# Input transfers of 88 and 40 rows padded to 96 and 48, in a one-core mLSTM and MoE kernel with a planned instruction order

## The chip, the core and the metric

The kernel runs on one core of a Trainium2 chip. It is one launch; the metric is the device time of that launch in microseconds (us). A profiled execution gives, beside its time, the span from its first to its last instruction.

## What is computed

The reference is a chain of an mLSTM layer (32 heads of 40 dimensions, 768 steps, 4 batches) and two feed-forward blocks on the 3,072 tokens that it yields.

```
for t in range(S):
    m_new = max(f_gate[t] + m, i_gate[t]); f_stab = exp(f_gate[t] + m - m_new); i_stab = exp(i_gate[t] - m_new)
    C = f_stab * C + i_stab * outer(v_t, k_t);  n = f_stab * n + i_stab * k_t
    y[t] = sigmoid(o_gate[t]) * (C q_t) / max(|n . q_t|, 1)
x = y as (3072, 320)
x = ((x @ w1) * (x @ w2)) @ w3 @ w_out                      # 320 -> 1024 -> 1024 -> 320
out = max(x @ v1, x @ v2, x @ v3) @ v_out                   # 320 -> 768 -> 320
```

Everything is float32 to the caller.

## The kernel before

**Work.** The recurrence is cut into nine chunks of 88 steps (the last has 64) per batch, and each chunk into two units of four heads: 72 units, `u` from 0 to 71. A unit loads keys and values (`kv`, line 490), values shifted for the carried state (`vs`, line 493), queries and keys for the scores (line 528 for the first `NP` = 10 units, tile `raw`; line 531 for the others, tile `misc` in the trace), queries for the carried state (`qq`, line 535) and a row of decays spread over the partitions (`dd`, line 538). Every second unit also loads output gates (`og`: line 462 for the first five chunks, tile `sg`; line 504 afterwards). GpSimd (POOL) and ScalarE (ACT) make the decay matrix `dd` (lines 544 to 552); TensorE makes scores (line 568 in the first ten units straight from `raw`, line 589 in the others from rounded halves); VectorE multiplies them with `dd` into `pk` (line 599); POOL or VectorE scales `qq` into rows 64 to 127 of `pk` (line 595); TensorE multiplies `pk` with `kv` (line 609). Rows 88 to 127 of a `kv` tile carry the state; columns 0 to 39 of these rows hold an identity, put into each of the three `kv` buffers once by the transfers of line 455 from `eyes`. Rows 64 to 127 of each `qq` and `vs` buffer are set to zero once.

**Weights.** The weights come as 64-bit floats and are turned into 32-bit ones on the chip, a piece of 128 x 512 at a time (`granule`, transfers of line 831, ACT lines 836, 842 and 853, VectorE lines 845 and 859). `w3 @ w_out` is folded into one matrix (line 909). The feed-forward steps are long rows of matmuls (lines 681 to 685 and 748 to 767) over blocks of 384 tokens.

**Order.** Nothing is issued in the order of the program text. `Plan.op` records each operation with its engine, an estimate of its duration, what it reads and what it writes; `Plan.run` works through a model of the engines and fixes one order for all of them. An operation's rank is its latest start plus a bias for its engine and the first tile it writes (`BIAS`, "Dkv" is a DMA into `kv`). All transfers are issued by SyncE (SP), one queue in order; in the model each takes 450 ns of SP, then its estimate times a factor on a common bus, and no transfer is issued while the bus is more than `AHEAD` = 2,500 ns ahead of the clock. The order on each engine is then fixed; on the chip an engine works through it and waits at each instruction for what that needs. Semaphore waits are put in for every pair of accesses to the same rows of a tile.

**Lines the change touches.** Lines 450 to 453 copy, by ACT, an identity into columns 176 to 215 of each of the three `raw0` buffers. In line 533 `rs`, the number of score rows, is 88 for all units (`Q0` holds units 2 to 17, and units 0 and 1 have 88 rows anyway), so the four matmuls of line 568 read the 88 key columns of `raw` and not the identity behind them. The transfer of line 528 fills columns 0 to 175 of each head's 216, so that its pieces lie apart in the tile: 704 bytes each, four per partition.

Of the kernel before, what the change touches and what calls it, by code (L numbers as in the profile page):

```python
# [8 lines left out]
F32 = mybir.dt.float32  # L9
# [19 lines left out]
Q0 = tuple(range(2, 18))  # L29
# [20 lines left out]
BIAS = {"Add": -69250, "Aev": -20750, "Ag": -87500, "Akst": -433250, "Aph": -85750, "Aqs": -169250,  # L50
        "Araw0b": -112500, "Asa": 80250, "Asg": 77000, "Astg": 121500, "Asx": 172500, "Awa": 53750,
        "Awar": -227750, "Awb": -299750, "Awc": -44250, "Awcr": -22750, "Awd": -95750, "Axh": -106000,
        "Dcs": -153000, "Ddd": 56000, "Ddna": 41500, "Dev": 135250, "Dg": -568250, "Dkv": 58750,
        "Dkvb": -138750, "Dqq": -150000, "Draw": 61250, "Dsg": -172250, "Dstg": 56250, "Dsx": -253500,
        "Dvs": 54000, "Gdd": 165250, "Gg": 165750, "Gmp": -83500, "Gpk": -8500, "Gpl": 102000, "Gqqb": -89000,
        "Gqs": -328250, "Gvsb": -67000, "Gwa": 248750, "Gwar": 130750, "Gwc": 173750, "Gwcr": 276500,
        "Gwd": 10000, "Gy": -204000, "Pac0": 26000, "Pac1": -256750, "Pac2": -108750, "Po": -750, "Ppt": 32000,
        "Ps": -74250, "Pwk": 16250, "Pxt": -36000, "S-": -191250, "Sg": -328500, "Vam": -7250, "Vev": 440250,
        "Vg": -40750, "Vkst": 79750, "Vkv": -170750, "Vmp": -182500, "Vpk": -130500, "Vsa": -42250,
        "Vsg": -18250, "Vstg": 206750, "Vsx": 16750, "Vwb": -33250, "Vxl": 65500, "Vy": -8500, "Vzero": -40750}  # L60
# [21 lines left out]
class Plan:  # L82
# [48 lines left out]
    def run(self):  # L131
# [70 lines left out]
        while events:  # L202
# [22 lines left out]
            for e, h in heaps.items():  # L225
                while h and free[e] <= t:
                    j = h[0][1]
                    if done[j]:
                        heapq.heappop(h)
                        continue  # L230
                    if e == "D" and bus > t + AHEAD:
                        push(-1, bus - AHEAD)
                        break
                    heapq.heappop(h)
                    done[j] = True
                    a = ops[j][0].index(e)
                    ns = ops[j][1][a]
                    order.append((t, j, ops[j][2][a]))
                    if e == "D":
                        free[e] = t + 450  # L240
                        bus = max(bus, t + 1300) + ns * 1.4
                        end = bus + 1200
                    elif e == "P":
                        free[e] = end = clock(t, ns, self.cols[j])
                        past.append((t, end, self.cols[j]))
                    else:
                        end = t + ns
                        if e == "G" or e == "V" and self.port[j]:
                            at = t + GRAB[e]
                            x, y = held["V" if e == "G" else "G"]  # L250
                            if x <= at < y:
                                end = y + ns - GRAB[e]
                            held[e] = (at, end)
                        free[e] = end
                    for key, s in touch[j]:
                        if key not in part:
                            part[key] = 0
                            use[s][0] += 1
                        part[key] += 1
                        use[s][1] = max(use[s][1], end + 250)  # L260
# [15 lines left out]
def mlstm_moe_kernel(  # L276
# [45 lines left out]
    for pool_, tag, bufs, n in (  # L322
# [3 lines left out]
        (tmp, "sx", EX, 1024), (tmp, "w3", L_BUFS, 512), (tmp, "raw0", RAW0, 4 * (128 + L)),  # L326
# [123 lines left out]
    eye = cs[0:40, 0:40].unsqueeze(1).to_broadcast([40, 4, 40])  # L450
    for i, t in enumerate(slots["raw0"]):
        P.op("A", act(160), lambda t=t: A.copy(out=view(t, [40, 4, 128 + L], F32)[:, :, 2 * L:128 + L], in_=eye),
             r=[("cs", 0)], w=[("raw0b", i)])
# [7 lines left out]
    for c in range(SIGN):  # L461
        dma(313, lambda c=c: SP.dma_start(out=sg0[0:L, c], in_=og[0, c]), w=[("sg", (0, c))])
        sig.append(P.op("A", 360 + (1283 if c == 0 else 0), lambda c=c: A.activation(
            out=sg0[0:L, c], in_=sg0[0:L, c], func=AF.Sigmoid
        ), w=[("sg", (0, c))]))
# [19 lines left out]
    def load(u):  # L485
# [4 lines left out]
        dma(317, lambda: SP.dma_start(out=T("kv", u)[0:L], in_=kv[b, g, c]), w=[("kv", u, "k")])  # L490
        if c:
            new(("vs", u), [128, 4, 41], F32, "vs")
            dma(44, lambda: SP.dma_start(out=T("vs", u)[64:L].rearrange("p a b -> p (a b)"), in_=vs[b, g, c]),
                r=[("vsb", turn["vs"] % len(slots["vs"]))], w=[("vs", u)])

    def gates(b, c):
# [25 lines left out]
    def unit(u):  # L522
# [3 lines left out]
        if u < NP:  # L526
            new(("raw", u), [40, 4, L + 128], F32, "raw0")
            dma(313, lambda: SP.dma_start(out=T("raw", u)[:, :, 0:2 * L], in_=qk0[g, c]), w=[("raw", u)])
        else:
            new(("raw", u), [120, 2, 4, L], F32, "raw")  # L530
            dma(939, lambda: SP.dma_start(out=T("raw", u), in_=qk[b, g, c]), w=[("raw", u)])
        rs = L if u >= NP or u in Q0 else r
        if rs < r:
            new(("qq", u), [128, 4, L], F32, "qq")
            dma(157, lambda: SP.dma_start(out=T("qq", u)[L:128], in_=qk[b, g, c, 0:40, 0]),
                r=[("qqb", turn["qq"] % len(slots["qq"]))], w=[("qq", u)])
        new(("dd", u), [128, 4, n], F32, "dd")
        dma(501, lambda: SP.dma_start(
# [24 lines left out]
        if u < NP:  # L563

            def f():
                raw = T("raw", u)
                for h in range(4):
                    PE.matmul(T("s", u)[:rs, h], lhsT=raw[:, h, L:L + rs], rhs=raw[:, h, 0:n], start=True, stop=True)

            P.op("P", 870 if rs == 128 else 640, f, r=[("raw", u), ("raw0b", u % RAW0)], w=[("s", u)])  # L570
# [21 lines left out]
        if rs < r:  # L592
# [7 lines left out]
            out=T("pk", u)[:rs, :, 0:n], in0=T("s", u)[:rs], in1=T("dd", u)[:rs], op=ALU.mult  # L600
# [217 lines left out]
    def granule(src, dst=None):  # L818
# [12 lines left out]
        dma(n * 2.844, lambda: SP.dma_start(out=tl().rearrange("p a b -> p (a b)"), in_=src.bitcast(I32)),  # L831
# [218 lines left out]
def _lay(i):  # L1050
# [9 lines left out]
    qk0 = qk0.reshape(2, NCH, D, 4, 2 * L)  # L1060
    qk = np.concatenate([qk, qk[:, :, :, 0:24], qk, qk[:, :, :, 24:40]], 3)
    kvt = np.zeros((B, 2, NCH, L, 4, 81), f)
    kk = k.reshape(B, 2, 4, S, D).transpose(0, 1, 3, 2, 4)
    vv = v.reshape(B, 2, 4, S, D).transpose(0, 1, 3, 2, 4)
    kvt[:, :, :, :, :, 80] = 1.0
# [4 lines left out]
    og = np.zeros((B, NCH, L, DM), f)  # L1070
# [55 lines left out]
```

## Time and profile before

| | |
|---|---|
| median of 3 runs | 735.6 us (735.3 to 739.76) |
| the profiled execution | 736.07 us |
| its span | 733.5 us |
| TensorE (PE) busy | 693.9 us, 95% of the span |
| weight loads (PEld) / VectorE (DVE) / ACT / POOL busy | 667.0 / 493.4 / 361.3 / 359.8 us |
| moved by DMA | 80.43 MB |

The page gives busy time by engine and 40 slices of the span, then the DMA queues, the chain of work that ended last, and the costliest groups of instructions. Views of the trace ask the same of a stretch, a line or a tile. A wait is the idle time of an engine before an instruction, with the event that ended it. The granted clock is TensorE's: 1.00 stands for 2.4 GHz, 0.50 for 1.2 GHz, and a value between is a mean over a stretch that holds both.

### The profile page before, as it was taken

The numbers are of one execution on the slowest core, as the hardware profiler recorded it, in microseconds if no ns is written. First come the engines' busy times: TensorE is split into PE (matmuls) and PEld (weight loads), VectorE is DVE, ScalarE is ACT, GpSimd is POOL, SyncE is SP. The second block draws the span as 40 slices with busy tenths as digits, with TensorE's granted clock in tenths as the row PEclk, the third lists the DMA queues.
The fourth block names the chain that finished last, engine by engine and source line by source line (L and its number), as shares of the span: only waits on it lengthen the run. The fifth ranks groups of instructions, "written<-read, shape, count | busy, mean of one in ns | idle before, by whom it ended". The sixth has DMA issues, their size and how long they took to land.

```text
span 733.5 us, 12870 instructions
## 1 busy us (share of the span) xinstructions
PE 693.9 (95%) x4269; PEld 667.0 (91%) x4269; DVE 493.4 (67%) x1202; ACT 361.3 (49%) x722; POOL 359.8 (49%) x494
## 2 busy tenths in 40 slices
PE   0788799999999999999999999999999999999998
PEld 0576787889899999999999999999999999999997
DVE  6578798897887788677575687776476783233333
ACT  7769799978984334353242334453233232322221
POOL 2587587877746457765342467865144441000000
PEclk9968799999999999999999999999999999999999
DMA  6887678765542435432221354433032320000000
GB/s 193 253 236 223 204 192 234 225 202 149 170 144 79 111 89 156 109 100 81 61 59 46 107 127 133 121 103 85 11 84 82 89 69 1 1 0 1 1 28 27
DMA packets 50994, 80.43 MB, mean 110 GB/s; under 512 B 10881, under 2 KB 37153, under 8 KB 50929
## 3 DMA queue, kind: packets, MB, share of 16 engines
q1 hardware_dynamic: 50928, 79.62, 38.6%
q8 instruction: 33, 0.54, 0.3%
q14 instruction: 33, 0.26, 0.1%
HBM read 75.57 MB, written 4.03 MB: 109 GB/s over the span
## 4 chain that ended last, share of the span: by engine, by line
PE 79%; DVE 7%; ACT 7%; issue 2%; DMA 2%; POOL 1%; SPq 1%; DVEq 0%; ACTq 0%; POOLq 0%
PE wk L681 12%; PE wk L683 12%; PE wk L682 12%; PE ac L767 8%; PE aq L609 6%; PE wk L685 6%; PE wk L684 6%; PE ac L748 4%; PE ac L752 4%; PE wk L909 3%; PE ac L750 2%; PE aq L589 2%; ACT stg L853 2%; PE aq L649 1%; ACT stg L836 1%
## 5 line engine op out<-in xcount | busy, mean ns | idle before, releaser
L697 ACT CAST ph<-pr 128x384 fp32r<-128x384 f32 (+1 forms) x114 | 58.0, 510 | 115.2 <-PE ac L767 43.8
L701 POOL TENSOR_TENSOR pl<-pr,ph 128x384 fp32r<-128x384 f32 (+1 forms) x52 | 53.1, 1021 | 124.1 <-ACT ph L697 106.1
L732 DVE TENSOR_TENSOR pr<-pr,wk 128x384 f32<-128x384 f32 (+1 forms) x98 | 52.4, 537 | 70.1 <-PE wk L685 68.5
L681 PE MATMUL wk<-xh,wch 128*128 128x384 f32 x288 | 99.5, 345 | 0.0
L683 PE MATMUL wk<-xl,wch 128*128 128x384 f32 x288 | 97.0, 337 | 0.0
L682 PE MATMUL wk<-xh,wcl 128*128 128x384 f32 x288 | 96.9, 337 | 0.0
L681 PE MATMUL wk<-xh,wah 128*128 128x384 f32 x256 | 91.8, 359 | 1.8 <-ACT xh L660 1.8
L683 PE MATMUL wk<-xl,wah 128*128 128x384 f32 x256 | 87.3, 341 | 2.2 <-DVE xl L663 2.2
L682 PE MATMUL wk<-xh,wal 128*128 128x384 f32 x256 | 87.0, 340 | 0.0
L578 POOL TENSOR_TENSOR qs<-misc,qs 40x352 fp32r<-40x352 f32 (+1 forms) x62 | 63.1, 1018 | 40.3 <-ACT qs L574 34.6
L558 POOL TENSOR_TENSOR pk<-kv,dd 128x160 f32<-128x160 f32 (+1 forms) x64 | 38.4, 600 | 85.9 <-PE aq L609 78.4
L520 DVE RECIPROCAL misc<-misc 88x40 f32<-88x40 f32 x232 | 70.3, 357 | 5.1 <-POOL misc L516 4.4
L544 POOL TENSOR_TENSOR dd<-am,dd 128x352 f32<-128x352 f32 (+2 forms) x72 | 58.4, 811 | 23.7 <-DVE stg L845 11.4
L701 DVE TENSOR_TENSOR pl<-pr,ph 128x384 fp32r<-128x384 f32 (+1 forms) x62 | 37.4, 603 | 48.4 <-ACT ph L697 42.6
L714 ACT COPY pr<-wk 128x384 f32<-128x384 f32 x64 | 30.6, 478 | 77.2 <-PE wk L685 77.2
L552 ACT ACTIVATE dd<-dd 128x352 f32<-128x352 f32 (+2 forms) x72 | 35.5, 493 | 59.1 <-POOL dd L548 58.7
L609 PEld LDWEIGHTS aq<-kv,pk 128*128 128x128 f32 (+2 forms) x496 | 60.7, 187 | 3.9 <-issue 2.6
L609 PE MATMUL aq<-kv,pk 128*128 128x41 f32 (+2 forms) x496 | 59.5, 270 | 1.1 <-DVE misc L630 0.7
L635 POOL TENSOR_TENSOR misc<-misc 88x160 f32<-88x160 f32 (+1 forms) x62 | 36.5, 588 | 45.6 <-DVE misc L630 44.9
L681 PEld LDWEIGHTS wk<-xh,wch 128*128 128x128 f32 x288 | 54.4, 189 | 0.0
L682 PEld LDWEIGHTS wk<-xh,wcl 128*128 128x128 f32 x288 | 54.2, 188 | 0.0
L853 ACT ACTIVATE stg<-stg 128x512 f16<-128x512 f32 (+2 forms) x41 | 52.6, 1282 | 3.2 <-DVE stg L845 2.4
(135 smaller groups left out, 1755.9 us busy)
## 6 DMA issues: line engine op xcount, KB each, us to landing
misc<-in_qk SPq DMA_DIRECT2D x62, 330.0 KB
dd<-d_na SPq DMA_DIRECT2D x56, 176.0 KB
kv<-in_kv SPq DMA_DIRECT2D x72, 111.4 KB
stg<-in_w3t SPq DMA_DIRECT2D x13, 512.0 KB
stg<-in_wc SPq DMA_DIRECT2D x9, 512.0 KB
out<-misc SPq DMA_DIRECT2D x23, 160.0 KB
qq<-in_qk SPq DMA_DIRECT2D x64, 55.0 KB
misc<-in_og SPq DMA_DIRECT2D x31, 110.0 KB
```

What stands on the lines that cost most here:

```text
L520: P.op("V", 69 + 6.25 * DM / RCP, lambda sl=sl: V.reciprocal(out=T(*t)[:, sl], in_=T(*t)[:, sl]), w=[t])
L544: P.op("G", 735, lambda: G.tensor_tensor(out=T("dd", u)[:r], in0=am[:r, c, h0:h0 + 4].unsqueeze(2).to_broadcast([r, 4, n]), in1=T("dd", u) ...
L578: P.op("G", 889, lambda: G.tensor_tensor(out=T("qs", u)[0:40], in0=T("raw", u)[0:40, 0, :, 0:n], in1=T("qs", u)[0:40].bitcast(F32), op=ALU ...
L609: PE.matmul(T("o", u)[:m, h], lhsT=T("pk", u)[:r, h, 0:m], rhs=T("kv", u)[:r, h, 40:81], start=True, stop=True)
L681: PE.matmul(p, lhsT=h_[:, kt], rhs=xh[:, kt], start=kt == 0, stop=False)
L682: PE.matmul(p, lhsT=l_[:, kt], rhs=xh[:, kt], start=False, stop=False)
L683: PE.matmul(p, lhsT=h_[:, kt], rhs=xl[:, kt], start=False, stop=False)
L697: P.op("A", act(n), lambda sl=sl: A.copy(out=T("ph", key)[:, sl], in_=T(*src)[:, sl]), r=[src + part], w=[("ph", key) + part])
L701: e.tensor_tensor(out=T("pl", key)[:, sl], in0=T(*src)[:, sl], in1=T("ph", key)[:, sl].bitcast(F32), op=ALU.subtract)
L732: P.op("V", dve(sl.stop - sl.start), lambda ps=ps, sl=sl: V.tensor_tensor(out=T(*sc)[:, sl], in0=T(*sc)[:, sl], in1=T(*ps)[:, sl], op=ALU. ...
L767: PE.matmul(T(f"ac{m}", (k, 1)), lhsT=src[:, m * 128:m * 128 + 128], rhs=w[:, o:o + DM], start=first_, stop=last_,)
L853: A.activation(out=sign, in_=tl()[:, :, 1].bitcast(F32), func=AF.Copy)
```

## The change

Keys and values, and output gates, are laid out in HBM with 96 rows a chunk instead of 88, and moved as 96. Rows 88 to 95 of the key columns hold the first eight rows of the identity, the rest of the added rows is zero. The queries for the carried state are moved as 48 rows into partitions 80 to 127, instead of 40 rows into 88 to 127; the first eight are queries that are not used, and line 599 overwrites their products. Queries and keys of the first ten units are laid out with 48 rows (eight of them zero) and fill the tile without gaps, so that each partition's 2,816 bytes are one piece; the matmuls read rows 0 to 39. The identity columns of `raw` and their three ACT copies are gone. The planner's estimates of eight transfers change, its bus factor goes from 1.4 to 1.45, the estimate for the direct scores from 640 to 720 ns, and all biases have new values, so that the order of the instructions on every engine is made anew.

```diff
+LP = 96
-Q0 = tuple(range(2, 18))
-BIAS = {"Add": -69250, "Aev": -20750, "Ag": -87500, "Akst": -433250, "Aph": -85750, "Aqs": -169250,
...
+XFER = 1.45
+BIAS = {"Add": -85250, "Aev": -24000, "Ag": -123750, "Akst": -400000, "Aph": -83000, "Aqs": -186250,
...
-                        bus = max(bus, t + 1300) + ns * 1.4
+                        bus = max(bus, t + 1300) + ns * XFER
...
-        (tmp, "sx", EX, 1024), (tmp, "w3", L_BUFS, 512), (tmp, "raw0", RAW0, 4 * (128 + L)),
+        (tmp, "sx", EX, 1024), (tmp, "w3", L_BUFS, 512), (tmp, "raw0", RAW0, 8 * L),
...
-    eye = cs[0:40, 0:40].unsqueeze(1).to_broadcast([40, 4, 40])
-    for i, t in enumerate(slots["raw0"]):
-        P.op("A", act(160), lambda t=t: A.copy(out=view(t, [40, 4, 128 + L], F32)[:, :, 2 * L:128 + L], in_=eye),
-             r=[("cs", 0)], w=[("raw0b", i)])
...
-        dma(313, lambda c=c: SP.dma_start(out=sg0[0:L, c], in_=og[0, c]), w=[("sg", (0, c))])
+        dma(318, lambda c=c: SP.dma_start(out=sg0[0:LP, c], in_=og[0, c]), w=[("sg", (0, c))])
...
-        dma(317, lambda: SP.dma_start(out=T("kv", u)[0:L], in_=kv[b, g, c]), w=[("kv", u, "k")])
+        dma(322, lambda: SP.dma_start(out=T("kv", u)[0:LP], in_=kv[b, g, c]), w=[("kv", u, "k")])
...
-            dma(313, lambda x=x, t=t: SP.dma_start(out=T(*t), in_=og[b, x]), w=[t])
+            dma(318, lambda x=x, t=t: SP.dma_start(out=T(*t), in_=og[b, x]), w=[t])
...
-            new(("raw", u), [40, 4, L + 128], F32, "raw0")
-            dma(313, lambda: SP.dma_start(out=T("raw", u)[:, :, 0:2 * L], in_=qk0[g, c]), w=[("raw", u)])
+            new(("raw", u), [48, 4, 2 * L], F32, "raw0")
+            dma(333, lambda: SP.dma_start(out=T("raw", u), in_=qk0[g, c]), w=[("raw", u)])
...
-            dma(939, lambda: SP.dma_start(out=T("raw", u), in_=qk[b, g, c]), w=[("raw", u)])
-        rs = L if u >= NP or u in Q0 else r
-        if rs < r:
+            dma(888, lambda: SP.dma_start(out=T("raw", u), in_=qk[b, g, c]), w=[("raw", u)])
+        if L < r:
...
-            dma(157, lambda: SP.dma_start(out=T("qq", u)[L:128], in_=qk[b, g, c, 0:40, 0]),
+            dma(174, lambda: SP.dma_start(out=T("qq", u)[80:128], in_=qk[b, g, c, 56:104, 0]),
...
-        dma(501, lambda: SP.dma_start(
+        dma(464, lambda: SP.dma_start(
...
-                    PE.matmul(T("s", u)[:rs, h], lhsT=raw[:, h, L:L + rs], rhs=raw[:, h, 0:n], start=True, stop=True)
+                    PE.matmul(T("s", u)[:L, h], lhsT=raw[0:40, h, L:2 * L], rhs=raw[0:40, h, 0:n], start=True, stop=True)
...
-        dma(n * 2.844, lambda: SP.dma_start(out=tl().rearrange("p a b -> p (a b)"), in_=src.bitcast(I32)),
+        dma(n * 2.484, lambda: SP.dma_start(out=tl().rearrange("p a b -> p (a b)"), in_=src.bitcast(I32)),
...
+    qk0 = np.concatenate([qk0, np.zeros((2, NCH, 48 - D, 4, 2 * L), f)], 2)
...
-    kvt = np.zeros((B, 2, NCH, L, 4, 81), f)
+    kvt = np.zeros((B, 2, NCH, LP, 4, 81), f)
+    kvt[:, :, :, L:LP, :, 0:40] = eye[0:LP - L, None]
...
-    og = np.zeros((B, NCH, L, DM), f)
+    og = np.zeros((B, NCH, LP, DM), f)
```

## Rows read from the trace of the kernel before

**Rows 1.** Windows of the span: busy time by engine, granted clock, DMA share, GB/s.
```profile
0.00:21.60 21.60, 1.15 (x10) 1.05 (x10) 13.43 (x24) 15.71 (x24) 6.80 (x20) 1.00 0.70 201
21.60:44.00 22.40, 18.45 (x102) 14.97 (x102) 14.43 (x41) 15.36 (x23) 13.83 (x21) 0.97 0.79 239
44.00:54.00 10.00, 9.51 (x45) 8.53 (x45) 7.41 (x21) 7.28 (x12) 8.12 (x13) 0.50 0.87 253
54.00:78.00 24.00, 18.12 (x87) 12.49 (x85) 19.86 (x43) 21.84 (x37) 16.33 (x23) 0.86 0.75 222
78.00:88.20 10.20, 10.20 (x43) 10.20 (x43) 6.80 (x15) 5.90 (x11) 3.70 (x6) 0.55 0.62 184
88.20:98.40 10.20, 10.20 (x68) 10.04 (x68) 9.16 (x18) 10.15 (x19) 8.83 (x10) 1.00 0.65 199
98.40:225.00 126.60, 121.87 (x720) 110.67 (x718) 110.79 (x255) 112.13 (x206) 93.67 (x113) 1.00 0.66 189
225.00:734.00 509.00, 504.36 (x3206) 499.02 (x3205) 311.48 (x791) 172.88 (x397) 208.51 (x294) 1.00 0.26 69
```

**Rows 2.** The chain that ended last, first 22 us: start us, duration, what.
```profile
1.65 4.44 DMA sx<-in_wo
...
6.43 0.95 SPq L455
...
9.12 2.32 DMA misc<-in_og
...
15.98 0.36 SPq L831
...
17.20 4.34 DMA raw<-in_qk
```

**Rows 3.** Waits, 21.6 to 98.4 us: us in total, times, longest.
```profile
PE aq L568 <- DMA raw<-in_qk: 11.6, 3, 11.1
...
POOL pk L558 <- DMA kv<-in_kv: 4.1, 2, 2.6
```

**Rows 4.** The chain that ended last, 42 to 53 us.
```profile
42.03 1.23 POOL dd L548
...
44.95 1.35 ACT sx L853
...
51.87 1.17 POOL dd L548
```

**Rows 5.** DMA of the whole span, from the page.
```profile
q1 hardware_dynamic: 50928, 79.62, 38.6%
```

**Rows 6.** DMA of the first 70 us: packets, MB, share; issues with KB each.
```profile
q1 hardware_dynamic: 9827, 16.24, 78.1%
...
kv<-in_kv SPq DMA_DIRECT2D x13, 111.4 KB
raw<-in_qk SPq DMA_DIRECT2D x10, 110.0 KB
...
sg<-in_og SPq DMA_DIRECT2D x5, 110.0 KB
qq<-in_qk SPq DMA_DIRECT2D x10, 55.0 KB
...
misc<-in_og SPq DMA_DIRECT2D x2, 110.0 KB
```

**Rows 7.** Issue times on SP by line, ns: min/median/max, first and last start.
```profile
L528 SPq DMA_DIRECT2D raw<-in_qk x10: 791/796/812, 17.2 to 55.6; - x10
```

**Rows 8.** The same view for line 531: 120 rows of 2,816 bytes.
```profile
L531 SPq DMA_DIRECT2D misc<-in_qk x62: 324/325/1380, 58.3 to 587.1; - x62
```

**Rows 9.** ACT between 6 and 17 us: start, us, instruction, idle before it.
```profile
9.29 0.76 ACT L452 COPY raw<-cs 40x160 f32<-40x160 f32 x3
9.96 1.18 ACT L463 ACTIVATE sg<-sg 88x320 f32<-88x320 f32 x3
11.53 1.28 ACT L514 ACT_TABLE_LOAD   x1 [0.39 <-DMA misc<-in_og]
```

More of the change, by code (lines that the diff above doesn't have):

```diff
@@ L49 @@
 GRAB = dict(V=140, G=177)
-BIAS = {"Add": -69250, "Aev": -20750, "Ag": -87500, "Akst": -433250, "Aph": -85750, "Aqs": -169250,
[L51 to L60, printed above, removed]
+XFER = 1.45
+BIAS = {"Add": -85250, "Aev": -24000, "Ag": -123750, "Akst": -400000, "Aph": -83000, "Aqs": -186250,
+        "Asa": 46250, "Asg": 75500, "Astg": 120750, "Asx": 264500, "Awa": 57000, "Awar": -160000,
+        "Awb": -243000, "Awc": 53000, "Awcr": -54750, "Awd": -140250, "Axh": -104250, "Dcs": -94750,
+        "Ddd": 48500, "Ddna": 43250, "Dev": 129500, "Dg": -537000, "Dkv": 63500, "Dkvb": -72250,
+        "Dqq": -168750, "Draw": 57250, "Dsg": -175250, "Dstg": 51750, "Dsx": -234250, "Dvs": 50000,
+        "Gdd": 155750, "Gg": 174250, "Gmp": -53250, "Gpk": -9750, "Gpl": 55000, "Gqqb": -84250, "Gqs": -343250,
+        "Gvsb": 22500, "Gwa": 211000, "Gwar": 177000, "Gwc": 104000, "Gwcr": 247000, "Gwd": 35000,
+        "Gy": -155000, "Pac0": 27750, "Pac1": -280250, "Pac2": -143750, "Po": -2250, "Ppt": -38250,
+        "Ps": -154250, "Pwk": 16250, "Pxt": -59250, "S-": -204750, "Sg": -320000, "Vam": -41500, "Vev": 472750,
+        "Vg": -85500, "Vkst": 84750, "Vkv": -143750, "Vmp": -152750, "Vpk": -81250, "Vsa": -45250, "Vsg": 8500,
+        "Vstg": 130500, "Vsx": -10500, "Vwb": -25000, "Vxl": 30500, "Vy": -16000, "Vzero": 55750}
 TICK = 10240 / 3
@@ L461, in mlstm_moe_kernel @@
     for c in range(SIGN):
-        dma(313, lambda c=c: SP.dma_start(out=sg0[0:L, c], in_=og[0, c]), w=[("sg", (0, c))])
+        dma(318, lambda c=c: SP.dma_start(out=sg0[0:LP, c], in_=og[0, c]), w=[("sg", (0, c))])
         sig.append(P.op("A", 360 + (1283 if c == 0 else 0), lambda c=c: A.activation(
-            out=sg0[0:L, c], in_=sg0[0:L, c], func=AF.Sigmoid
+            out=sg0[0:LP, c], in_=sg0[0:LP, c], func=AF.Sigmoid
         ), w=[("sg", (0, c))]))
@@ L489, in load @@
         new(("kv", u), [128, 4, 81], F32, "kv")
-        dma(317, lambda: SP.dma_start(out=T("kv", u)[0:L], in_=kv[b, g, c]), w=[("kv", u, "k")])
+        dma(322, lambda: SP.dma_start(out=T("kv", u)[0:LP], in_=kv[b, g, c]), w=[("kv", u, "k")])
         if c:
             new(("vs", u), [128, 4, 41], F32, "vs")
-            dma(44, lambda: SP.dma_start(out=T("vs", u)[64:L].rearrange("p a b -> p (a b)"), in_=vs[b, g, c]),
+            dma(60, lambda: SP.dma_start(out=T("vs", u)[64:L].rearrange("p a b -> p (a b)"), in_=vs[b, g, c]),
                 r=[("vsb", turn["vs"] % len(slots["vs"]))], w=[("vs", u)])
@@ L502, in gates @@
         for x, t in zip(cs_, toks):
-            new(t, [L, DM], F32, "og")
-            dma(313, lambda x=x, t=t: SP.dma_start(out=T(*t), in_=og[b, x]), w=[t])
+            new(t, [LP, DM], F32, "og")
+            dma(318, lambda x=x, t=t: SP.dma_start(out=T(*t), in_=og[b, x]), w=[t])
         if grp:
@@ L567, in f @@
                 for h in range(4):
-                    PE.matmul(T("s", u)[:rs, h], lhsT=raw[:, h, L:L + rs], rhs=raw[:, h, 0:n], start=True, stop=True)
-            P.op("P", 870 if rs == 128 else 640, f, r=[("raw", u), ("raw0b", u % RAW0)], w=[("s", u)])
+                    PE.matmul(T("s", u)[:L, h], lhsT=raw[0:40, h, L:2 * L], rhs=raw[0:40, h, 0:n], start=True, stop=True)
+            P.op("P", 720, f, r=[("raw", u)], w=[("s", u)])
         else:
@@ L591, in unit @@
             P.op("P", 390, f, cols=90, r=[("qs", u), ("kst", u % 2)], w=[("s", u)])
-        if rs < r:
+        if L < r:
             def scaled(e):
@@ L599, in unit @@
         P.op("V", dve(4 * n), lambda: V.tensor_tensor(
-            out=T("pk", u)[:rs, :, 0:n], in0=T("s", u)[:rs], in1=T("dd", u)[:rs], op=ALU.mult
+            out=T("pk", u)[:L, :, 0:n], in0=T("s", u)[:L], in1=T("dd", u)[:L], op=ALU.mult
         ), r=[("s", u), ("dd", u)], w=[("pk", u, 1)])
@@ L1060, in _lay @@
     qk0 = qk0.reshape(2, NCH, D, 4, 2 * L)
+    qk0 = np.concatenate([qk0, np.zeros((2, NCH, 48 - D, 4, 2 * L), f)], 2)
     qk = np.concatenate([qk, qk[:, :, :, 0:24], qk, qk[:, :, :, 24:40]], 3)
-    kvt = np.zeros((B, 2, NCH, L, 4, 81), f)
+    kvt = np.zeros((B, 2, NCH, LP, 4, 81), f)
+    kvt[:, :, :, L:LP, :, 0:40] = eye[0:LP - L, None]
     kk = k.reshape(B, 2, 4, S, D).transpose(0, 1, 3, 2, 4)
     vv = v.reshape(B, 2, 4, S, D).transpose(0, 1, 3, 2, 4)
-    kvt[:, :, :, :, :, 80] = 1.0
+    kvt[:, :, :, 0:L, :, 80] = 1.0
     for c in range(NCH):
```

## The prediction

> **What bounds the kernel now.** I read the windows first. From 225 us on, PE is busy 504.4 of 509 us at full clock while the DMA engines are busy 26% of the time [rows 1]: this part is bound by PE's own matmuls, the change alters none of them, and a transfer that lands earlier has nothing to shorten. I leave it as it is. What can move lies ahead of that: 20.5 us without PE up to 21.6 us, 10.3 us of PE idle between 21.6 and 98.4 us (76.8 us less 18.45, 9.51, 18.12, 10.20 and 10.20), 4.7 us between 98.4 and 225 us, and PE time at the lower clock level (0.50 from 44 to 54 us, a mean of 0.55 from 78 to 88.2 us) [rows 1].
>
> Then the chain. Up to 21.6 us it is made of transfers and of SP's queue: a weight piece that takes 4.44 us, the identity transfers, an output gate that takes 2.32 us, ACT's gate work, and `raw`, issued at 17.20 us and landed after 4.34 us; PE's first score waits for that `raw` for 11.1 us, which is the longest of its waits [rows 2, 3]. After that no transfer stands on the chain for long: from 42 to 53 us POOL's work on `dd` and ACT's work on weights take turns [rows 4], although the DMA engines are busy 79%, 87% and 75% of these stretches [rows 1]. So transfers set the start, and later they only feed engines that are themselves nearly full.
>
> **How a transfer is spread.** The queue of the whole span moved 50,928 packets [rows 5]. The rows and pieces of the kernel's 463 transfers add up to 44,912; 6,016 packets are left, 13 per transfer. That remainder comes out exactly if a transfer runs on as many of the 16 engines as the largest divisor of its row count not above 16, and each of these ends it with one packet: 140 transfers of 128 or 32 rows on 16, 116 of 88 rows on 11, 62 of 120 rows on 15, 77 of 40 rows on 10, 64 of 24 rows on 12, 4 of 8 rows on 8. So 88 rows are eight to an engine on 11 engines, and 96 rows six to an engine on 16.
>
> The price of a byte: in the first 70 us the queue held 16 engines for 78.1% of the time and moved 16.24 MB [rows 6], 0.781 x 16 x 70 / 16.24 = 53.9 engine-us per MB, or 53.9 ns for a KB on one engine. By this, on the engines that carry most: `kv` 8 x 1,296 bytes, 0.56 us, becomes 6, 0.42 us; a gate 8 x 1,280, 0.55, becomes 0.41 us; `qq` 4 x 1,408, 0.30, becomes 3, 0.23 us; `raw` 16 pieces of 704, 0.61, becomes 3 of 2,816, 0.46 us.
>
> **The change part by part.**
>
> *The start.* `raw` is issued as 40 x 4 pieces in 796 ns [rows 7]; pieces that fill a partition, 120 of them, are issued in 325 ns [rows 8]. I take 325 for the new `raw`: -0.47 us on the chain. Its transfer saves 0.15 and the gate ahead of it 0.14 us, since both stand on the chain [rows 2]. Together -0.8 us. Ends: -0.5 (the issue alone) and -2.5 (the landing falls to the gate's 2.32 us as well).
>
> *21.6 to 98.4 us.* 13 `kv`, 7 gates, 10 `qq` and 10 `raw` of the first 70 us [rows 6] save 13 x 0.14 + 7 x 0.14 + 10 x 0.08 + 10 x 0.15 = 5.1 us on the fullest engines, and SP 10 x 0.47 = 4.7 us of issue between 17 and 56 us. Waits that these transfers end are 0.5 us at PE (11.6 less 11.1) and 4.1 us at POOL [rows 3]; POOL is on the chain, but not all the time. I take -1.2 us, about a quarter of the 4.6 us. Ends: nothing, where each wait is filled by the engine's next work (POOL is 50 to 80% busy [rows 1]), and -5.1 us, where the fullest engines set the pace.
>
> *From 98.4 us.* The same saving per unit, but PE is busy 121.9 of 126.6 us and the DMA engines 66% [rows 1]: nothing. The cover is PE's own queue; without it, some 5 us would be there at most (17 more `kv`, 16 `qq`, 8 gates, by the prices above).
>
> *ACT's three copies.* 0.76 us at 9.29 us, 0.95 with the overlap counted apart. Behind the next sigmoids ACT waits 0.39 us for the gate transfer in any case [rows 9], so their removal gives nothing; where the gate lands 0.14 us earlier the wait is still there. Without that cover it would be 0.8 us.
>
> *Added bytes.* 8 more rows for each of 72 `kv`, 36 gates, 64 `qq`, 10 `raw`, some 2 MB on 80: they go to the engines that had less, and are counted in the per-engine prices above. DVE and PE do the same instructions on the same shapes.
>
> *The new order.* This is the largest and the least known term. In the plan a weight piece cost 512 x 2.844 x 1.4 = 2.04 us of bus, and now 1.84; by the price above, 32 KB on an engine are 1.77 us. `kv` stood at 0.44 and now 0.47, against 0.56 before and 0.42 now; `raw` at 0.44 and now 0.48, against 0.61 and 0.46; `dd` (8 x 1,408) at 0.70 and now 0.67, against 0.61. Before, some terms were 15% too high and others 21 to 28% too low; now all are 4 to 11% too high. The rule that holds transfers back by 2,500 ns of bus then works on times that agree with the chip, and SP's 450 ns per issue is no longer exceeded by `raw`. What a better order can win is PE's 10.3 idle us, and the half clock of 78 to 88.2 us, where PE is busy all the time: 10.2 x (1 - 0.55) = 4.6 us [rows 1]. Of these 14.9 us I take a sixth, -2.5 us, because the biases were remade throughout and a new order can lose as well. Ends: -7.5 us (half of it) and +4.6 us (another such stretch at the lower clock).
>
> Sum: 0.8 + 1.2 + 2.5 = 4.5 us. The span goes from 733.5 to 729.0 us; with the 2.6 us that the profiled execution spends around its span (736.07 - 733.5), 731.6 us. Against the median of the runs, 0.5 us under the profiled execution, 731.1; I say 731 us.
>
> **The rivals.**
>
> *The balance counts in full (about 722.5 us).* The fullest engines set the pace up to 98 us: -2.5, -5.1 and some -5.5 us of the order, 13.1 us together. For it: 87% as a mean over 16 engines with many transfers confined to 10 or 11 leaves the first ten hardly a pause [rows 1]. Against it: the chain names POOL, ACT and DVE there [rows 4].
>
> *The padding does not shorten a transfer (about 735 us).* If what a transfer's end waits for is the way into the tile's rows and not the engines, then the rows that share a way are as many as before, and 16 engines only queue where 11 queued; the issue's 0.47 us is left, 735.1 us. For it: landings of 2.32 to 4.44 us are many times the 0.4 to 1.8 us that the bytes take [rows 2]. Against it: a DMA share that reaches 87% [rows 1] says the engines themselves are full. The Trainium skill, "SBUF — State Buffer", section "Door 1: The DMA port swizzle", states such a rule: partitions 0 to 63 reach only eight of 16 ports and 32 to 63 share those of 0 to 31. By it the fullest port takes eight rows of an 88-row and of a 96-row tile alike, and the forecast's terms of the start and the middle would shrink to the issue; no row here splits the share by port.
>
> *The new order loses the clock (about 742 us, slower).* Where ACT and DVE fall behind with weights, PE pauses and is granted the lower level; so it was from 78 us, after 5.9 idle us between 54 and 78 us [rows 1]. Each 10 us of full PE work at that level cost 4.6 us. Should the order push PE's pauses beyond 98 us, where before all was at 1.00, two such stretches add 9.2 us, and with nothing won but the start, 735.6 - 0.8 + 9.2 = 744; with one, 739. It decides against the change from the first 10 us of busy PE time at 0.50 beyond what is there now.
>
> *The identity comes too late (738 to 743 us).* `kv` now writes rows 88 to 95, which the transfers of line 455 write too, so a buffer's first `kv` transfer has to wait for its identity to land, at the head of SP's only queue, with every transfer behind it. Before, the last identity was issued at 9 us and the first `kv` at 16.4 us, far apart [rows 2]. If the new order puts one right behind the other, a landing of 2.3 to 4.4 us is added up to three times. It decides where the two are less than that landing apart.
>
> **How the numbers follow.** Forecast 0.44 (726 to 736 us), balance in full 0.20, no shorter transfer 0.19, clock lost 0.12, identity late 0.05. A measurement of this kernel tells 1% from nothing, that is under 728.2 or over 743 us. Faster by over 1%: all of the second and a third of the first, 0.35. Slower: two thirds of the last two, 0.12. Within 1%: 0.53. The range 721 to 742 us leaves a few hundredths below, and most of the slower cases above.
>
> **What would show it.** Start: `raw` issued in about 0.33 us, its first landing under 4 us, PE's first score before 21.6 us. Spread: the queue's packets go from 50,928 to 50,928 + 108 x 13 + 64 x 14 - 10 x 106 = 52,168. Middle: POOL's 4.1 us for `kv` shrink, the DMA share of the first 70 us falls below 0.78 for more bytes. Order: PE idle of 21.6 to 98.4 us below 10.3, and the lower clock level shorter. After 225 us no change: if the tail from the same work on differs by over 2 us, I have misread the bound. SP waiting for a landing at the first `kv` would be the last rival.

## The result, and the profile after

| | before | changed | e1 (old order, padded) |
|---|---|---|---|
| median of the runs, us | 735.97 (734.49 to 740.0, 11 runs) | 742.66 (739.37 to 744.25, 11 runs) | 734.88 (733.24 to 736.76, 7 runs) |
| ratio to before, 95% interval | | 1.0079 [1.0058, 1.0099] | 0.9971 [0.9941, 1.0001] |
| span of the profiled execution, us | 733.5 | 741.3 | 732.8 |
| granted clock, mean | 0.981 | 0.977 | 0.981 |

The change makes the kernel 0.8% slower, 5.8 us by the ratio. The forecast was 731 us, 0.7% faster; sign and size are wrong, and the time lies 0.7 us above the range. The third column is the experiment that says why: the same padded transfers in the order of before are not slower at all.

First the page of the changed kernel: span, busy time by engine, the transfer queue, and the chain that ended last.

```profile
span 741.3 us, 12914 instructions
...
PE 695.3 (94%) x4269; PEld 667.3 (90%) x4269; DVE 503.7 (68%) x1196; ACT 363.4 (49%) x716; POOL 369.6 (50%) x503
...
q1 hardware_dynamic: 52168, 81.69, 39.7%
...
PE 75%; DVE 11%; DMA 6%; issue 4%; POOL 3%; ACT 1%; SPq 0%; POOLq 0%; DVEq 0%; ACTq 0%
```

The same last line of the page before:

```profile
PE 79%; DVE 7%; ACT 7%; issue 2%; DMA 2%; POOL 1%; SPq 1%; DVEq 0%; ACTq 0%; POOLq 0%
```

VectorE and transfers hold more of the chain now, ACT and PE less. The queue moved 52,168 packets, exactly what the spread over 16 engines had to give. PE does the same 4,269 matmuls. VectorE and GpSimd are each busy some 10 us longer than before with practically the same work.

The windows of the changed kernel, columns as in [rows 1]:

```profile
0.00:21.60 21.60, 1.14 (x9) 1.03 (x9) 13.56 (x23) 15.10 (x21) 7.79 (x21) 1.00 0.75 213
21.60:44.00 22.40, 18.05 (x84) 13.52 (x85) 12.23 (x33) 17.24 (x21) 9.22 (x12) 0.89 0.88 242
44.00:54.00 10.00, 9.20 (x47) 6.98 (x46) 6.40 (x17) 6.37 (x11) 7.14 (x12) 0.67 0.85 245
54.00:78.00 24.00, 19.11 (x100) 14.32 (x100) 21.62 (x50) 20.07 (x36) 21.66 (x30) 0.78 0.81 225
78.00:88.20 10.20, 7.24 (x36) 6.95 (x36) 9.95 (x16) 8.19 (x15) 10.05 (x11) 0.73 0.72 192
88.20:98.40 10.20, 9.21 (x53) 9.19 (x54) 9.93 (x19) 7.39 (x14) 8.65 (x12) 0.83 0.85 276
98.40:225.00 126.60, 118.71 (x688) 107.51 (x686) 114.94 (x246) 107.33 (x195) 89.93 (x110) 0.99 0.63 181
225.00:734.00 509.00, 508.66 (x3235) 504.05 (x3234) 312.28 (x792) 180.85 (x406) 214.70 (x300) 1.00 0.27 72
```

Beside [rows 1]: PE stands idle 14.0 us instead of 10.3 between 21.6 and 98.4 us, and 7.9 instead of 4.7 up to 225 us. Busy time multiplied by one minus the granted clock, stretch by stretch, gives 13.9 us lost to the lower level, 12.4 before (coarse, since the clock has two digits). So 3.7 + 3.2 + 1.5 = 8.4 us are lost, against 7.8 us of span. Between 78 and 88.2 us DVE and POOL are now busy nearly all the time and PE is not; before it was the other way round. Behind 225 us PE is busy all the time, only later: the first output transfer is issued 9.8 us later than before, the last 8.1 us.

PE's longest waits of the changed kernel from 98.4 to 225 us (us in total, times, longest):

```profile
PE aq L605 <- DVE xl L659: 2.8, 2, 1.9
PE ac L748 <- DVE pl L697: 2.0, 1, 2.0
PE aq L585 <- DVE misc L626: 1.1, 1, 1.1
```

The longest of these waits before:

```profile
PE ac L752 <- DVE pl L701: 1.2, 1, 1.2
```

They name VectorE. Its weight steps last longer. The next two fences are the groups of VectorE in the first 225 us (count | busy, mean ns of one), of the changed kernel and then of e1, where line 860 is what is 855 here:

```profile
L855 DVE SCALAR_TENSOR_TENSOR stg<-stg 128x512 int32<-128x512 int32 x15 | 17.1, 1146 | 0.2
L855 DVE SCALAR_TENSOR_TENSOR w<-stg 128x512 int32<-128x512 int32 x13 | 13.3, 1032 | 2.4 <-ACT stg L849 2.4
```

```profile
L860 DVE SCALAR_TENSOR_TENSOR stg<-stg 128x512 int32<-128x512 int32 x16 | 13.3, 831 | 3.7 <-ACT stg L854 3.5
L860 DVE SCALAR_TENSOR_TENSOR w<-stg 128x512 int32<-128x512 int32 x13 | 10.2, 786 | 4.0 <-ACT stg L854 3.8
```

The same instruction on the same shape takes 1.15 us in the new order and 0.83 us in the old. That is a symptom; what it costs is asked below.

### The profile page after: what moved, and what is told of

Its sections match the earlier page's. It is cut to its first block, busy times and chain, and to the rows that moved or that the text cites. A ratio compares the mean times of both kernels' runs of the same rounds, so it can differ in the third digit from the quotient of the medians.

```text
span 741.3 us, 12914 instructions
## 1 busy us (share of the span) xinstructions
PE 695.3 (94%) x4269; PEld 667.3 (90%) x4269; DVE 503.7 (68%) x1196; ACT 363.4 (49%) x716; POOL 369.6 (50%) x503
## 2 busy tenths in 40 slices
DMA packets 52234, 82.50 MB, mean 111 GB/s; under 512 B 11864, under 2 KB 37912, under 8 KB 52168
## 3 DMA queue, kind: packets, MB, share of 16 engines
q1 hardware_dynamic: 52168, 81.69, 39.7%
## 4 chain that ended last, share of the span: by engine, by line
PE 75%; DVE 11%; DMA 6%; issue 4%; POOL 3%; ACT 1%; SPq 0%; POOLq 0%; DVEq 0%; ACTq 0%
PE wk L677 12%; PE wk L678 11%; PE wk L679 11%; PE ac L763 9%; PE wk L681 6%; PE wk L680 6%; PE aq L605 5%; PE ac L744 4%; PE ac L748 4%; PE ac L746 3%; DMA stg<-in_w3t 2%; PE aq L585 2%; PE wk L905 1%; DVE stg L855 1%; DVE kst L578 1%
## 5 line engine op out<-in xcount | busy, mean ns | idle before, releaser
L697 POOL TENSOR_TENSOR pl<-pr,ph 128x384 fp32r<-128x384 f32 (+1 forms) x47 | 49.0, 1043 | 127.6 <-ACT ph L693 107.1
L697 DVE TENSOR_TENSOR pl<-pr,ph 128x384 fp32r<-128x384 f32 (+1 forms) x67 | 44.7, 667 | 47.4 <-ACT ph L693 46.9
L517 DVE RECIPROCAL misc<-misc 96x40 f32<-96x40 f32 x232 | 71.0, 357 | 3.7 <-POOL misc L513 2.8
L712 DVE TENSOR_TENSOR pr<-pr,wk 128x384 f32<-128x384 f32 x64 | 34.8, 544 | 42.6 <-PE wk L681 41.6
L725 ACT COPY pr<-wk 128x384 f32<-128x384 f32 x48 | 22.9, 478 | 77.0 <-PE wk L681 77.0
L710 ACT COPY pr<-wk 128x384 f32<-128x384 f32 x64 | 30.7, 480 | 59.3 <-PE wk L681 59.2
```

What stands on the lines that cost most here:

```text
L517: P.op("V", 69 + 6.25 * DM / RCP, lambda sl=sl: V.reciprocal(out=T(*t)[:, sl], in_=T(*t)[:, sl]), w=[t])
L697: e.tensor_tensor(out=T("pl", key)[:, sl], in0=T(*src)[:, sl], in1=T("ph", key)[:, sl].bitcast(F32), op=ALU.subtract)
```

## The experiments

All kernels compute the same. Where nothing else is said, a ratio is to the kernel before, timed beside it.

**Order or transfers?** e1 has every padded transfer, and the biases, estimates and bus factor of before, so that the order is that of before. e2 is the mirror, the order of the changed kernel with the old transfers. e1b and e1c split e1.

```diff
 e1 (from before)
+LP = 96
-dma(317, lambda: SP.dma_start(out=T("kv", u)[0:L], in_=kv[b, g, c]), ...
+dma(317, lambda: SP.dma_start(out=T("kv", u)[0:LP], in_=kv[b, g, c]), ...
...
 e2 (from the changed kernel)
-LP = 96
+LP = 88
-new(("raw", u), [48, 4, 2 * L], F32, "raw0")
+new(("raw", u), [40, 4, L + 128], F32, "raw0")
...
 e1b: of e1 only raw;   e1c: of e1 only kv, gates and qq
```

> All padded transfers and the contiguous raw of the changed kernel, with the estimates and biases of the kernel before, so that every engine runs the old order (three ACT copies less). Theory 'the order costs the time': 736 us less what the transfers give, 731 to 736 us, PE's first score before 21.6 us and raw landing in under 4.3 us. Theory 'the padded transfers cost the time' (each now ends with the last of 16 engines, and 2 MB more are moved): 740 to 745 us, with kv landings longer than before.

> The changed kernel with its own order, but 88 and 40 rows and raw in 160 pieces as before. Theory 'the order': 742 to 748 us, as slow as the changed kernel or slower, since raw is issued in 0.8 us again and the fullest engines carry more. Theory 'the padded transfers': 735 to 738 us.

> The old order, with the contiguous raw of 48 rows alone; kv, gates and qq keep 88 and 40 rows. Theory 'the order': 0.5 to 1.5 us under the kernel before, by raw's shorter issue (0.8 to 0.33 us) at the start. Theory 'the padded transfers': the same or up to 2 us slower.

> The old order, with kv and gates of 96 rows and qq of 48, raw as before in 160 pieces. Theory 'the order': 0 to 3 us under the kernel before. Theory 'the padded transfers': 3 to 7 us over it, with longer landings of kv.

| | us | ratio to before |
|---|---|---|
| e1, old order, padded | 734.88 | 0.9971 [0.9941, 1.0001] |
| e2, new order, not padded | 744.47 | 1.0093 [1.0061, 1.0124] |
| e1b, old order, raw alone | 735.97 | 0.9982 [0.9963, 1.0001] |
| e1c, old order, rows alone | 736.86 | 1.0019 [0.9992, 1.0046] |

The order costs the same with and without padding: 1.0079 against 0.9971, 1.0093 against 1. The padded transfers give between nothing and 0.6%; of their two halves neither can be told from zero. The queue of e1's first 70 us, beside [rows 6], shows that the forecast's prices were too good:

```profile
q1 hardware_dynamic: 9037, 16.61, 85.2%
```

The engines are held 85.2% of the time instead of 78.1% for 2% more bytes: 57 engine-us per MB, where [rows 6] gave 54. The same transfers in the same order give 55 and 57 in h1 and h3 (below). By the packet records of e1 and of before, in the first 70 us a packet of 1,296 bytes lasts 79 ns on average (72 before), one of 1,280 bytes 74 (63), one of 1,408 bytes 93 (80). So `kv` goes from 8 x 72 = 0.58 us to 6 x 79 = 0.47 us on its engines, a gate from 0.50 to 0.44, and `dd`, whose spread is as it was, from 8 x 80 = 0.64 to 0.74 us. The price of a byte was no constant: it rose where more transfers ran on 16 engines. How it rose by size, one execution does not tell: h1 and h3 have 75 and 81 ns for 1,296 bytes and 86 and 92 for 1,408, and e1b has 81 ns for 1,296 bytes although its `kv` is not padded. The gate's packets of 1,280 bytes are longer in each of the four kernels with padded gates in the old order (72 to 74 ns, against 63 and 64 in before and e1b).

**What of the order?** e5 asks whether the late start of `kv` does it: in the changed kernel the first `kv` is issued at 24.75 us, before at 16.38. e3 asks whether the choice between VectorE and GpSimd does it.

```diff
 e5 (from the changed kernel)
+first = [x for x in order if key(x[1]) in [("kv", u, "k") for u in range(3)]]
+order[at:at] = first      # right behind the first three dd transfers
 e3 (from the changed kernel)
+FORCE = {('pk', 11, 1): 'V', ...}      # 34 operations on the engine they had before
+to = FORCE.get(self.keys[j]) ...
```

> The changed kernel with one edit of its order: the first three kv transfers are issued behind the first three dd transfers, ahead of the weight piece at which SP waits at 13.5 us, instead of from 24.75 us on. Theory 'the start': the first product of pk and kv comes 8 to 11 us earlier, the lag of 3 us that the changed kernel has at 98 us goes, 738 to 740 us. Theory 'collisions': up to 1 us better, 741 to 743 us.

> The changed kernel with its own order, but 34 instructions of the first 235 us that either VectorE or POOL can do (pk, pl and the low halves of weights) go to the engine that did them in the kernel before, at the same places of the order. Theory 'collisions' (in the new order VectorE's instructions with two operands in SBUF run beside more of POOL's, and last longer: the 512-wide step of a weight piece 1.15 us instead of 0.85): VectorE's times fall back, 736 to 740 us. Theory 'the start' (the first kv comes 8 us later): 741 to 744 us. Theory 'the order as a whole': any value from 738 to 748.

e5: 745.18 us, 1.0116 [1.0086, 1.0147]. e3: 743.85 us, 1.0101 [1.0059, 1.0144]. Neither gives anything back. In e5 the early `kv` pushed `raw` back: its first issue moved from 16.64 to 18.03 us and PE's first score from 21.61 to 23.24, so e5 shows no net gain, and not that a late `kv` is free. VectorE's time over the shortest of each kind of instruction (one line, its tiles and its shape), added up over the first 225 us, is 29 us before, 28 in e1, 43 in the changed kernel and 39 in e3; the 27 and 40 in a text below are an earlier count of the same. With the engines exchanged the order stretches VectorE's instructions almost as much. Nor does the time follow that sum: it is 34 us in f1 and e7 below and 38 in f2, and they take 742, 748 and 757 us.

**The estimates, the biases, or their fit?** e6 and e7 pair the new estimates with the old biases, and the other way round. f1 to f4 are four new orders, all with padded transfers: biases fitted again, with the old estimates (f1, f2) and with the new (f3, f4), until the planner's own span was about that of before.

```diff
 e6: BIAS = that of before     e7: XFER = 1.4, dma(317, ...), dma(313, ...), ... = those of before
 f1 to f4: BIAS = values of a new fit
```

> The changed kernel with the biases of the kernel before; estimates and bus factor stay new. Theory 'the new biases cost the time': 733 to 738 us. Theory 'the new estimates cost it': 741 to 745 us. Under 'collisions' the time goes with VectorE's stretch over its shortest times in the first 225 us, 27 us before and 40 us in the changed kernel.

> The changed kernel with the estimates and the bus factor of the kernel before; the biases stay new. Theory 'the new biases': 740 to 746 us. Theory 'the new estimates': 734 to 738 us. Where both this and the last are as slow as the changed kernel or slower, it is that biases and estimates do not fit each other, and an order is no better than its chance.

> All padded transfers, old estimates and bus factor, and biases fitted anew to them from another start, so that the planner's own span is 706.6 us (706.9 for the kernel before, 707.1 for the changed one, 713.3 and 719.1 for the two mixed ones). On the chip the spans were 26.6 us above the planner's for the kernel before, 27.2 for old estimates with new biases, 34.2 for the changed kernel and 33.3 for new estimates with old biases. Theory 'the new estimates make the planner too hopeful': chip span 733 to 735, time 735 to 738 us. Theory 'an order is chance, the kernel before was a lucky one': anything from 735 to 750.

> As the last, a second fit to the old estimates, planner's span 707.4 us. Theory 'the new estimates': chip span 734 to 736, time 736 to 739 us. Theory 'chance': 735 to 750, and not the same distance from the planner's span as the last.

> All padded transfers, new estimates and bus factor, biases fitted to them from the old biases as a start; planner's span 706.9 us. Theory 'the new estimates make the planner too hopeful': chip span 740 to 742, time 742 to 745 us. Theory 'chance': 735 to 750.

> As the last, fitted from the new biases further down; planner's span 705.5 us. Theory 'the new estimates': chip span 739 to 740, time 741 to 743 us. Theory 'chance': 735 to 750.

| | estimates | planner's own span, us | measured, us | ratio to before |
|---|---|---|---|---|
| before | old | 706.9 | 736 | |
| changed | new | 707.1 | 742.66 | 1.0079 [1.0058, 1.0099] |
| e6 | new | 713.3 | 749.93 | 1.0184 [1.0147, 1.0221] |
| e7 | old | 719.1 | 748.0 | 1.0161 [1.0123, 1.0199] |
| f1 | old | 706.6 | 741.81 | 1.0054 [1.0023, 1.0086] |
| f2 | old | 707.4 | 757.31 | 1.0268 [1.0227, 1.0309] |
| f3 | new | 706.9 | 752.12 | 1.0202 [1.0148, 1.0257] |
| f4 | new | 705.5 | 740.84 | 1.0047 [1.0022, 1.0072] |

I had thought that one set of estimates makes the planner too hopeful by a fixed amount. The table refutes it: six orders that the planner puts within 2 us of each other (705.5 to 707.4) take 736 to 757 us, good and bad ones in either set. The order of before is the best of all eight. The planner's span says nothing about differences as small as those at stake here.

**Where is it lost?** The two orders can be spliced: the first operations in the order of one kernel, all the others in the order of the other. All four splices have the padded transfers.

```diff
+FIRST = (3, 6, 0, 32, 31, 1, ...)      # 553 (h1), 566 (h2) or 1,253 operations (h3, h4), in the other kernel's order
+head = set(FIRST)
+order = [... for j in FIRST] + [x for x in order if x[1] not in head]
```

> All transfers padded. The first 553 of the 3,218 operations stand in the order of the kernel before (what its planner issues up to about 98 us on the chip), the others in the order of the changed kernel. The old order alone with these transfers took 734.9 us, the new order alone 742.7. Theory (each stretch costs what its own order costs; PE's idle time grew by 3.7 us up to 98 us and by 3.2 us up to 225 us): about 739 us, the part up to 98 us won back. Rival (what is put off in the first 98 us is paid later, so that the start decides): about 735 us. Second rival (an order works only as a whole, a seam costs): 743 us or more.

> The mirror: the first 566 operations in the order of the changed kernel, the others in the order of before, all transfers padded. Theory (each stretch for itself): about 738 to 739 us. Rival (the start decides): about 743 us. Second rival (a seam costs): 743 us or more here and in the mirror alike.

> The first 1,253 operations in the order of before (up to about 220 us on the chip), the others in the order of the changed kernel, all transfers padded. Theory (everything is lost ahead of 225 us; from there the lag of the changed kernel stays at 8 us): about 735 us. Rival (the later order costs too, hidden in a lag that looks constant): 738 us or more.

> The mirror: the first 1,253 operations in the order of the changed kernel, the others in the order of before, all transfers padded. Theory (everything is lost ahead of 225 us): about 743 us. Rival (the later order costs too): 740 us or less.

I had set the seams by the planner's time (96 and 215 us); on the chip they lie later than the texts above say: the scores of unit 15, the last ahead of the first seam, run at 107 to 110 us, those of unit 28, just behind the second, at 239 to 253 us. The last columns are how far TensorE is behind the profiled execution of before where it has done the same part of its matmul work (each matmul counted by its time at full clock). They come from one execution each: e1c, in the old order too, is 4.3 us behind at 98 us in its own, so the argument rests on the times, and the lags show where.

| order | us | ratio to before | behind at 98 us | 152 us | 204 us | 723 us |
|---|---|---|---|---|---|---|
| h3: old to 240 us, then new | 734.98 | 0.9983 [0.9966, 0.9999] | -0.1 | -0.2 | -1.3 | -0.9 |
| h2: new to 110 us, then old | 738.12 | 1.0033 [1.0016, 1.0051] | 4.4 | 4.0 | 2.6 | 2.8 |
| h1: old to 110 us, then new | 743.32 | 1.0108 [1.0065, 1.0151] | 1.5 | 6.8 | 7.6 | 6.4 |
| h4: new to 240 us, then old | 744.75 | 1.0117 [1.0089, 1.0144] | 3.6 | 7.5 | 10.1 | 10.3 |
| changed kernel | 742.66 | 1.0079 [1.0058, 1.0099] | 3.3 | 6.7 | 9.5 | 8.1 |

From 240 us on the two orders are worth the same. That holds for these two and not for any order: f2 is 5 to 7 us behind at 204 us and 23 us at 723 us, with PE idle 10.0 us between 225 and 600 us, where before it was 0.5. The new order up to 110 us costs some 3 us (h2 against h3: 738.12 - 734.98), the stretch from 110 to 240 us the larger part, whatever ran ahead of it (h1 against h3: 8.3 us by the medians, 7.3 by the lags; h4 against h2: 6.6 and 7.5). It shows in PE's busy time between 98.4 and 225 us, first of h1, then of h3:

```profile
98.40:225.00 126.60, 117.65 (x689) 105.41 (x689) 116.13 (x251) 108.02 (x197) 89.87 (x110) 1.00 0.66 190
```

```profile
98.40:225.00 126.60, 122.57 (x725) 111.64 (x725) 112.41 (x257) 113.18 (x208) 95.36 (x113) 1.00 0.69 193
```

PE is idle 9.0 us in h1 and 4.0 us in h3, at full clock in both, and gets through 689 matmuls instead of 725. This is where the prediction's rival of the clock had looked for a loss; what is lost there is waiting, not clock.

**One place.** One of PE's waits in the changed kernel ends at 198.29 us. The timeline around it, of VectorE, then GpSimd, then PE (start us, us, engine, line, operation; in brackets the wait and what ended it):

```profile
194.33 3.91 DVE L697 TENSOR_TENSOR pl<-pr,ph 128x384 fp32r<-128x384 f32 x1
...
193.61 1.26 POOL L574 TENSOR_TENSOR qs<-misc,qs 40x352 fp32r<-40x352 f32 x1
194.84 1.30 POOL L868 TENSOR_TENSOR wcl<-stg,wch 128x512 fp32r<-128x512 f32 x1
196.11 0.99 POOL L697 TENSOR_TENSOR pl<-pr,ph 128x384 fp32r<-128x384 f32 x1
197.06 0.77 POOL L540 TENSOR_TENSOR dd<-am,dd 128x352 f32<-128x352 f32 x1
197.90 0.70 POOL L544 TENSOR_SCALAR_AFFINE_SELECT dd<-dd 88x352 f32<-88x352 f32 x1
...
198.29 0.80 PE L748 MATMUL ac<-pl,wb 128*128 128x384 f32 x3 [2.04 <-DVE pl L697]
```

The `pl` instruction, whose shortest take 0.49 us, ends 0.4 us after the fourth of four two-operand instructions that GpSimd runs without a pause, and PE waits 2.04 us for it. In e2, e5, h1 and h4, where the same stretch runs in the same order, it lasts 3.92 to 3.94 us. The Trainium skill, "SBUF — State Buffer", section "Who interferes with whom", states that a VectorE instruction with two inputs in SBUF contends with a GpSimd instruction that reads SBUF, not with one that only writes. This row agrees, and adds that the wait can go through several such instructions; the planner's model (`held`) ends it with the first. VectorE instructions that last over 1.5 us longer than the shortest of their kind, in the first 225 us: one before (1.6 us in total over the shortest), one in e1, four in the changed kernel (84.1, 94.5, 111.6 and 194.3 us; 9.5 us), four in e2 (9.9 us). k1 and k2 put an instruction that only writes into GpSimd's row at the four places.

```diff
+GAP = (426, 429, 556, 1235)
 for t, j, fn in order:
     fn()
+    if j in GAP:
+        self.gap()
+gap = big.tile([128, 32], F32, name="gap")      # k2: [128, 384]
+P.gap = lambda: G.memset(gap, 0.0)
```

> The changed kernel in its own order, with four short instructions of GpSimd that touch one operand only (a memset of 128x32, about 0.1 us each) put between its two-operand instructions at the four places where VectorE's two-operand instruction lasted over 1.5 us longer than its shortest (84.1, 94.5, 111.6 and 194.3 us; 2.55, 2.79, 2.78 and 3.91 us, 9.5 us over the shortest together; in the kernel before there is one such place, of 1.6 us). Theory (VectorE finds no room while GpSimd goes from one two-operand instruction straight to the next, and the new order makes such rows more often): these four instructions fall to under 2 us each, and 742.7 us falls by 2 to 5 us, since TensorE waited 2.0 us behind the last of them alone. Rival (such a wait only takes the place of another, as the choice of engines did in an earlier run): 742 to 744 us with the four instructions shorter. Second rival (a short gap is no room): the four instructions stay as long as they were.

> As the run before with four gaps, but each gap is a memset of 128x384; by the memset of 64x352 that lasted 0.36 us in the trace it takes about 0.4 us, where the short one took 0.12 us and left three of the stalls as they were (2.90, 2.14 and 4.01 us). Theory (VectorE finds no room in an unbroken row of two-operand instructions of GpSimd, and this makes a part of the loss): these three fall to under 1.6 us and the time to about 738 to 740 us, against 741.6 with short gaps and 742.7 without. Rival (the stalls are not what costs the time): they fall, and the time stays within 741 to 744 us. Second rival (a gap without two operands is no room however long): they stay, and so does the time.

k1 with gaps of 0.12 us: 741.61 us, 1.0061 [1.0036, 1.0085]. Three stalls stayed, this one too:

```profile
195.44 4.01 DVE L702 TENSOR_TENSOR pl<-pr,ph 128x384 fp32r<-128x384 f32 x1
...
195.93 0.11 POOL L1049 MEMSET gap<- 128x32 f32 x1
...
199.50 0.80 PE L753 MATMUL ac<-pl,wb 128*128 128x384 f32 x3 [1.51 <-DVE pl L702]
```

k2 with gaps of 0.42 us: 741.28 us, 1.0075 [1.0045, 1.0104]; its profiled execution has a span of 738.1 us. Here VectorE got through:

```profile
193.55 1.42 DVE L702 TENSOR_TENSOR pl<-pr,ph 128x384 fp32r<-128x384 f32 x1
195.00 2.50 DVE L583 TENSOR_TENSOR kst<-misc,kst 40x352 fp32r<-40x352 f32 x1
...
194.04 0.42 POOL L1049 MEMSET gap<- 128x384 f32 x1
194.42 1.73 POOL L873 TENSOR_TENSOR wcl<-stg,wch 128x512 fp32r<-128x512 f32 x1
```

`pl` falls from 3.91 to 1.42 us, PE's wait on it from 2.04 to 0.3 us, and k2's lag at 204 us is 6.0 us where the changed kernel had 9.5. But the next instruction, `kst`, now stands for 2.50 us, the stall at 111.6 us stays (3.13 us, with a gap of 0.41 us beside it), and the medians of k2 and of the changed kernel can't be told apart. That the row makes PE's wait at this place is shown by one execution of k2 against six with the stall; that these stalls make the 8 us is not. Orders without many of them are slow as well (e6 and f4 have one, e7 two).

## Why the prediction was wrong, point by point

- **The spread: right.** 52,168 packets, as worked out. The rule behind it is stated by the Trainium skill, "DMA: Bandwidth & Descriptors", section "Why a DMA increments its semaphore by 16 and not by 1" (the largest number up to 16 that divides the rows); both packet counts agree with it.
- **The start, -0.8 us: the issue right, the gain absent.** The issue times of `raw` (ns, least/median/most), beside [rows 7]:

```profile
L525 SPq DMA_DIRECT2D raw<-in_qk x10: 310/391/426, 16.6 to 55.4; - x10
```

  The first takes 0.34 us instead of 0.80 and starts 0.56 us earlier, yet PE's first score starts at 21.61 us, before at 21.58. In the old order it starts at 21.2 to 21.7 us with the short issue (e1, e1b, h1, h3) and at 21.2 us with the long one (e1c). The packet records show the reason: the first packet of `raw` starts 1.83 to 1.89 us after the start of the issue in those four, 1.85 and 2.05 us after it with the long issue (e1c and before), and 2.6 us after it in the changed kernel. I counted the 0.47 us of issue as part of the chain, and it lay beside that delay.
- **The middle, -1.2 us: not shown where I put it.** e1 and h3 gain 0.3% [0.0, 0.6] and 0.2% [0.0, 0.3], 1 to 2 us, about the terms of start and middle together. But the signs that I had named did not come in e1: POOL waits longer for `kv` than the 4.1 us of [rows 3] (4.9 us in h3, 2.4 in e1c), the DMA share of the first 70 us is 0.85 and not below 0.78, and PE's idle time from 21.6 to 98.4 us is 11.0 us (10.0 in h3, 10.3 before):

```profile
POOL pk L559 <- DMA kv<-in_kv: 5.0, 2, 3.5
```

  In these executions e1 and h3 get ahead between 98.4 and 225 us, where I had expected nothing (PE idle 3.5 and 4.0 us, 4.7 before), so that the size agrees by luck. The prices per engine were too good: packets last 9 to 17% longer in e1. POOL is busy 36 to 87% of the stretches of [rows 1], and not 50 to 80%. The rival in which padding shortens nothing would have given 735.1 us for these transfers, and e1 can't tell the two apart.
- **ACT's copies, the added bytes and the stretch from 225 us: no loss, as forecast.** e1 drops the copies and its first score comes 0.06 us earlier, less than these starts differ between kernels of one order. VectorE's shapes were not quite the same, its gate instructions run over 96 rows, but at no cost: the 232 reciprocals take 71.0 us in all, before 70.3. From 240 us on the orders of before and after give the same (h3). f2 shows that this is no property of the stretch: another order can leave PE idle there.
- **The new order, -2.5 us with ends of -7.5 and +4.6: this step failed.** It measured +7.8 us (742.66 - 734.88) with padding and, by the ratio, +6.8 us without (e2): PE waited 3.7 us longer up to 98.4 us and 3.2 us longer up to 225 us instead of less, and the splices put the larger part behind 110 us. The argument was that estimates nearer to the trace make a better order and that its errors fall on either side of zero. The first half fell with f1 to f4; against the second stand seven remade orders, of which none reaches that of before. The end of +4.6 us was also too near: it allowed for one stretch at half clock and for no waiting.
- **The rivals.** "The new order loses the clock" came nearest with its 742 us, for another reason: the lower clock took 1.5 us more than before, PE's pauses 6.9 us. "The balance counts in full" can be ruled out: without its 5.5 us for the order it asks 7.6 us of e1, which gains 2, at most 4. "The identity comes too late" did not happen: SP's pause from 20.8 to 23.9 us stands ahead of a weight piece, with `kv` behind it at 24.75 us, and e5, which issues `kv` ahead of it, gains nothing.

What stays open is which single feature of the new order costs the time. It is spread over the stretch from 110 to 204 us (h1 falls 3.2 us further behind up to 121 us, 2.1 more up to 152 us, 0.8 more up to 204 us), and one wait in it is traced to its cause. Of the kernels tried, h3 (734.98 us) and e1 (734.88 us) are the fastest: the padded transfers under the old order, 0.2 to 0.3% ahead of before and 1% ahead of the changed kernel.

## What to carry to other kernels

Where a change remakes a fitted order of instructions, run it once under the old order as well: here 0.3% (0.0 to 0.6) gained by the transfers lay under 1% lost by the order. Do not credit a fresh order with a gain because its model has better figures; orders that the model held equal lay up to 21 us apart on the chip, and the one in use had been the best of eight. A count that comes out exactly (the packets) proves how work is spread, not what it saves.

## What the runs showed of the hardware that I had not expected

- Spreading transfers over more engines raised the price of a byte: 54 engine-us per MB in the first 70 us of the kernel before, 55 to 57 in three kernels with the padded transfers in the same order (e1, h1, h3). Packets of 1,280 bytes took 63 ns before and 72 to 74 in these.
- A transfer whose issue was 0.46 us shorter had its first packet no earlier: 1.83 to 1.89 us after the start of the issue at 0.34 us (four kernels), 1.85 and 2.05 us after it at 0.8 us (two).
- A VectorE instruction of 0.5 us stood for 3.91 us beside four GpSimd instructions in a row. A write-only GpSimd instruction of 0.12 us among them left it standing, one of 0.42 us let it through; at another place one of 0.41 us did not (3.13 us).
